# Loading the first group's keys of a fused attention and feed-forward kernel in two transfers

## The chip, the cores and the metric

The kernel runs on one core of a Trainium2 chip. The metric is the device time of one execution in microseconds (us). Beside it stands a profile of one execution, taken by the hardware profiler, whose span reaches from the core's first to its last instruction.

## The reference

Two stages, the second fed by the first. B, H, S, D are 8, 12, 448 and 64; the second stage has 3584 rows (8 x 448), a width of 768 (12 x 64) and a hidden width of 2048.

```python
scores = scale * np.matmul(q, k.transpose(0, 1, 3, 2)) - np.log(S)
attn = 1.0 / (1.0 + np.exp(-scores))
attn_out = np.matmul(attn, v)
x = attn_out.transpose(0, 2, 1, 3).reshape(B * S, H * D)
h = x @ w_in
out = (h * (1.0 / (1.0 + np.exp(-beta * h)))) @ w_out
```

Inputs and output are float32. The attention has no softmax: each score goes through a sigmoid by itself.

## The kernel before

Work is in groups of four heads, three groups a batch, 24 in all. A group's queries and keys lie in a tile `raw` of 128 partitions: each of the four heads owns 32 partitions, and each partition holds 14 consecutive rows of 64 values ("blocks", NB = 14). VectorE (DVE) transposes these in squares of 32 x 32 into `qT` (L200) and `kT` (L212); TensorE (PE) makes scores from them (L229), ScalarE (ACT) puts the sigmoid on them (L242, L257), PE multiplies with the values (L335), DVE copies the result to `xT` (L349), and the feed-forward layers follow from there, partly as sums of products with fewer multiplications (L379, L410, L524, L652). Results leave by SyncE's queue (L711). The order of instructions on every engine is written out by hand: the lists LOADS, LATER, BEGIN (L811 to L881) and UNITS set it.

Nearly all loads are issued by GpSimd (POOL), which also converts float32 to float16 on the way (L125, L154, L169). The exception is group 0, whose keys and first half of the queries go as float32 on SyncE's (SP's) queue into `staged`, a piece of the later tile `gt` that is still free (L820 to L827): keys first, 14 blocks of 64 float32 values in each of 128 partitions, 448 KB, then 7 blocks of queries, 224 KB. The third transfer on that queue is beta, 8 KB (L856). At the same time POOL begins with the list LOADS: keys of group 1, the other half of group 0's queries, queries of group 1, values and so on.

BEGIN then has, in this order: the cast of key blocks 0 to 7 to float16 on DVE (L835), of key blocks 8 to 13 on ACT (L833) and of the 7 query blocks on ACT (L833); on DVE the key transposes, one over blocks 0 to 7 and one over blocks 8 to 13 (L212), and the transpose of the first half of the queries (L200); on PE 20 matmuls on a zeroed tile that compute nothing of use ("idle", L849), then the scores of group 0 for the first half of the queries, with further such matmuls between ("busy", L854). The DVE transposes of beta (L868) stand behind the queries of group 1.

The split of the keys at block 8 is that of `rows_of`:

```python
def rows_of(i: int):
    n = JF + int(i < KL // BLK)
    return i * JF + min(i, KL // BLK), n
```

With JF = 3 and KL // BLK = 2, `rows_of(0)` is (0, 4): four blocks from block 0.

Of the kernel before, what the change touches and what calls it, by code (L numbers as in the profile page):

```python
# [13 lines left out]
def kernel(  # L14
# [14 lines left out]
    B, H, S, D = q.shape  # L29
# [4 lines left out]
    HQ = P // BLK  # L34
    NB = S // BLK
# [106 lines left out]
# [4 lines that stand above are left out]
# [644 lines left out]
    NH = NB // 2  # L790
    share_psum(3)
    with tc.manual_schedule():
# [27 lines left out]
        staged = gt[:, 0:4].rearrange("p c w -> p (c w)").bitcast(FP32)  # L820
        raws[0] = rawp.tile([P, 2, NB, D], FP16, tag="raw", name="raw")
        parts = {1: (staged, NB), 0: (staged[:, NB * D :], NH)}
        for r, (to, n) in parts.items():
            nc.sync.dma_start(
                out=to[:, 0 : n * D],
                in_=(q, k)[r][0, 0:HQ].rearrange("h (p c) d -> (h p) (c d)", c=NB)[:, 0 : n * D],
            )  # L827

        def cast(r: int, c0: int, c1: int, act: bool):
# [234 lines left out]
```

## Time and profile before

| what | value |
|---|---|
| time, median of 3 runs | 369.52 us (369.27 to 369.52) |
| time of the profiled execution | 369.46 us |
| its span | 367.7 us |
| PE busy | 362.2 us, 99% |
| DVE busy | 262.7 us, 71% |
| ACT busy | 258.5 us, 70% |
| POOL busy | 83.4 us, 23% |
| moved by DMA | 34.62 MB, mean 94 GB/s |
| packets of POOL's queue (q0) | 26400, 40.5% of the 16 engines' span |
| packets of SyncE's queue (q1) | 5984, 11.6% of the 16 engines' span |

How to read it: the time holds some 1.8 us around the span. "Busy" counts the stretches in which an engine has an instruction under way; matmuls are pipelined, so a PE that is busy all the time is not one at its peak. L with a number is a line of the kernel. The DMA engines are shared: one transfer's rows are spread over all 16, and each row of a transfer is a packet or more.

### The profile page before, as it was taken

The numbers are of one execution on the slowest core, as the hardware profiler recorded it, in microseconds if no ns is written. First come the engines' busy times: TensorE is split into PE (matmuls) and PEld (weight loads), VectorE is DVE, ScalarE is ACT, GpSimd is POOL, SyncE is SP. The second block draws the span as 40 slices with busy tenths as digits, with TensorE's granted clock in tenths as the row PEclk, the third lists the DMA queues.
The fourth block names the chain that finished last, engine by engine and source line by source line (L and its number), as shares of the span: only waits on it lengthen the run. The fifth ranks groups of instructions, "written<-read, shape, count | busy, mean of one in ns | idle before, by whom it ended". The sixth has DMA issues, their size and how long they took to land.

```text
span 367.7 us, 7007 instructions
## 1 busy us (share of the span) xinstructions
PE 362.2 (99%) x2756; PEld 175.9 (48%) x2756; DVE 262.7 (71%) x487; ACT 258.5 (70%) x306; POOL 83.4 (23%) x125
## 2 busy tenths in 40 slices
PE   8999999999999999999999999999999999999996
PEld 4434444434444455544444455554444455555664
DVE  3548765688988867785675976779766677687664
ACT  5987976999777588876877759887777758870000
POOL 7525343311310023331131003337000012210000
PEclk9999999999999999999999999999999999999999
DMA  8999999955292110096379221004903030002332
GB/s 166 204 207 202 205 205 202 225 65 89 40 167 57 44 45 1 1 170 140 52 128 167 55 50 37 1 2 68 214 34 86 2 87 0 1 2 65 89 102 89
DMA packets 32416, 34.62 MB, mean 94 GB/s; under 512 B 9328, under 2 KB 28416, under 8 KB 32384
## 3 DMA queue, kind: packets, MB, share of 16 engines
q0 software_dynamic: 26400, 22.47, 40.5%
q1 hardware_dynamic: 5984, 11.71, 11.6%
q8 instruction: 21, 0.34, 0.4%
q14 instruction: 11, 0.09, 0.1%
HBM read 45.62 MB, written 11.01 MB: 154 GB/s over the span
## 4 chain that ended last, share of the span: by engine, by line
PE 92%; DMA 3%; DVE 2%; ACT 1%; issue 0%; DVEq 0%; ACTq 0%
PE ps L652 34%; PE ps L524 26%; PE ps L229 12%; PE ps L335 10%; PE ps L379 6%; PE ps L410 3%; DMA raw<-in_q_dram 2%; PE ps L854 1%; ACT attns L257 1%; DMA gt<-in_k_dram 1%; DVE w_S L484 1%; DVE gt L397 0%; ACT attns L242 0%; DVE qT L200 0%; ACT sg L396 0%
## 5 line engine op out<-in xcount | busy, mean ns | idle before, releaser
L257 ACT ACTIVATE attns<-ps,nlogs 128x1792 f16<-128x1792 f32 x73 | 128.0, 1754 | 41.0 <-PE ps L229 40.8
L652 PEld LDWEIGHTS <-sum 128*128 128x128 f16 x536 | 48.9, 98 | 42.1 <-issue 13.7
L652 PE MATMUL ps<-w_T,sum 128*128 128x384 f16 (+2 forms) x328 | 58.1, 319 | 0.0
L538 POOL TENSOR_TENSOR gt<-attns,sg 128x448 f16<-128x448 f32 x21 | 23.9, 1137 | 146.0 <-ACT sg L535 146.0
L229 PE MATMUL ps<-qT,kT 32*128 32x448 f16 (+3 forms) x800 | 50.5, 353 | 1.1 <-ACT attns L242 0.5
L535 ACT ACTIVATE sg<-ps,beta_sb 128x448 f32<-128x448 f32 x72 | 45.1, 630 | 8.6 <-PE ps L524 5.9
L524 PE MATMUL ps<-xT,w_in 128*128 128x448 f16 x216 | 49.2, 353 | 0.0
L524 PE MATMUL ps<-xT,w_S 128*128 128x448 f16 x216 | 49.2, 352 | 0.0
L538 DVE TENSOR_TENSOR gt<-ps,sg 128x448 f16<-128x448 f32 x72 | 44.3, 619 | 2.3 <-ACT sg L535 2.2
L349 DVE CAST xT<-ps 128x448 f16<-128x448 f32 (+1 forms) x50 | 27.9, 599 | 25.2 <-PE ps L335 25.2
L671 DVE TENSOR_TENSOR osb<-ps,osb 128x384 f32<-128x384 f32 (+2 forms) x67 | 36.1, 540 | 12.1 <-PE ps L652 10.5
L524 PEld LDWEIGHTS <-w_in 128*128 128x128 f16 x288 | 28.0, 98 | 26.6 <-issue 0.7
L379 PE MATMUL ps<-xT,w_in 128*128 128x448 f16 x192 | 40.0, 353 | 0.0
L335 PE MATMUL ps<-attns,v 128*64 128x448 f16 (+3 forms) x400 | 39.9, 353 | 0.0
L638 DVE TENSOR_TENSOR sum<-gt 128x1024 f16<-128x1024 f16 x57 | 38.4, 690 | 0.2
L652 PE MATMUL ps<-w_out,sum 128*128 128x384 f16 x208 | 37.9, 327 | 0.0
L652 PE MATMUL ps<-w_out,gt 128*128 128x384 f16 (+2 forms) x200 | 36.6, 320 | 0.0
L585 DVE TENSOR_TENSOR ps<-ps,attns 128x448 f32<-128x448 f32 x24 | 15.2, 633 | 24.1 <-PE ps L524 24.1
L524 PEld LDWEIGHTS <-w_S 128*128 128x128 f16 x216 | 21.1, 98 | 19.4
L125 POOL DMA_DIRECT2D raw<-in_q_dram x24 | 13.3, 555 | 67.7 <-DVE kT L212 53.2
L379 PEld LDWEIGHTS <-w_in 128*128 128x128 f16 x192 | 17.5, 98 | 21.2 <-issue 6.8
L335 PEld LDWEIGHTS <-v 128*64 128x64 f16 (+1 forms) x400 | 17.8, 108 | 20.4 <-issue 13.0
(57 smaller groups left out, 345.8 us busy)
## 6 DMA issues: line engine op xcount, KB each, us to landing
out_dram<-osb SPq DMA_DIRECT2D x98, 96.0 KB, 1.9
raw<-in_k_dram POOLq DMA_DIRECT2D x23, 224.0 KB, 6.5
raw<-in_q_dram POOLq DMA_DIRECT2D x23, 224.0 KB, 6.0
v<-in_v_dram POOLq DMA_DIRECT2D x16, 192.0 KB, 7.7
w_out<-in_moe_w_out_dram POOLq DMA_DIRECT2D x4, 768.0 KB, 17.9
v<-in_v_dram POOLq DMA_DIRECT2D x16, 144.0 KB, 8.0
w_in<-in_moe_w_in_dram POOLq DMA_DIRECT2D x3, 512.0 KB, 11.0
w_in<-in_moe_w_in_dram POOLq DMA_DIRECT2D x3, 256.0 KB, 11.4
```

Source lines behind the costliest of these rows:

```text
L229: nc.tensor.matmul(sco[base : base + nk, hh, u0 : u0 + n], kT[g][lo : lo + BLK, jt * P : jt * P + nk, e], qT[g][lo : lo + BLK, c0 : c0 + n ...
L257: nc.scalar.activation(out=attns[:, slot : slot + 2].rearrange("p n h s -> p (n h) s"), in_=sco, func=AF.Sigmoid, bias=nlogs[:, 0:1], scal ...
L335: nc.tensor.matmul(av[hh * D : (hh + 1) * D, 0:n], vs[b][base : base + nk, 2 * (s % NPAIR) + hh, jt], at[base : base + nk, hh, 0:n], start ...
L349: nc.vector.tensor_copy(out=xTs[b][:, s % NPAIR, c0 : c0 + n], in_=av)
L379: nc.tensor.matmul(m1, w_in16[:, hc, dc * P : (dc + 1) * P], xTs[b][:, hc], start=fresh, stop=(hc == hi - 1), skip_group_check=lo > 0,)
L524: nc.tensor.matmul(out, w[:, c, i * P : (i + 1) * P], m[:, c], start=(start and c == 0), stop=(c == KH - 1), skip_group_check=not start,)
L535: nc.scalar.activation(out=sg, in_=h, func=AF.Sigmoid, bias=0.0, scale=beta_sb[:, dc : dc + 1])
L538: return lambda: engine.tensor_tensor(out=gt[:, dc, b % 2 * S : b % 2 * S + S], in0=h, in1=sg, op=ALU.mult)
L585: nc.vector.tensor_tensor(out=D, in0=B, in1=p5, op=ALU.add)
L638: nc.vector.tensor_tensor(out=sums[t, i], in0=x, in1=y, op=op)
L652: nc.tensor.matmul(m2, (x if op is None else sums[t, i])[:, dc], w[:, dc, lo:hi], start=first, stop=(dc == ND - 1), skip_group_check=i >= 4,)
L671: nc.vector.tensor_tensor(out=out, in0=in0, in1=in1, op=op)
```

## The change

The keys' transfer is cut at block 8 (K0 = 2 x 4): 8 blocks (256 KB), then 6 blocks (192 KB), then the queries as before. All three are issued by SyncE, in this order, ahead of beta. Nothing else is edited; lines below it move down by one.

```diff
         parts = {1: (staged, NB), 0: (staged[:, NB * D :], NH)}
-        for r, (to, n) in parts.items():
+        K0 = 2 * rows_of(0)[1]
+        for r, c0, c1 in ((1, 0, K0), (1, K0, NB), (0, 0, NH)):
             nc.sync.dma_start(
-                out=to[:, 0 : n * D],
-                in_=(q, k)[r][0, 0:HQ].rearrange("h (p c) d -> (h p) (c d)", c=NB)[:, 0 : n * D],
+                out=parts[r][0][:, c0 * D : c1 * D],
+                in_=(q, k)[r][0, 0:HQ].rearrange("h (p c) d -> (h p) (c d)", c=NB)[:, c0 * D : c1 * D],
             )
```

The instructions that read these tiles stay in number and order. The waits follow the transfers: DVE's cast now waits for the first part of the keys, ACT's first cast for the second part.

## The prediction

> **What bounds the kernel now.** I read the page first, for who is busy, then the first 20 us of the timeline, because the edit touches nothing later, then the waits, and last the DMA view in narrow windows, because the edit changes only transfers.
>
> ```profile
> PE 362.2 (99%) x2756; PEld 175.9 (48%) x2756; DVE 262.7 (71%) x487; ACT 258.5 (70%) x306; POOL 83.4 (23%) x125
> PE ps L849 <- DVE gt L843: 1.2, 1, 1.2
> PE ps L229 <- ACT attns L242: 0.5, 1, 0.5
> PE ps L229 <- DVE qT L200: 0.4, 1, 0.4
> ```
>
> The page's first row has TensorE (PE) busy for 99% of the span. The other three rows are all of PE's waits in the whole trace: 2.1 us. Only one of them lies between the loads of group 0 and PE: the 0.4 us for the transposed queries. So the start of the first scores sets the time: what moves it moves the rest, unless something later absorbs it. The timeline of the start, in the order in which it is needed:
>
> ```profile
> 0.74 0.38 SPq L824 DMA_DIRECT2D gt<-in_k_dram  x1
> 1.18 0.42 SPq L824 DMA_DIRECT2D gt<-in_q_dram  x1
> 1.65 0.42 SPq L856 DMA_DIRECT2D beta_in<-in_moe_beta_dram  x1
> 1.29 0.72 POOL L125 DMA_DIRECT2D raw<-in_k_dram  x1 [0.42 <-issue]
> 1.19 4.27 PE L849 MATMUL ps<-gt 128*128 128x256 f16 x20 [1.19 <-DVE gt L843]
> 4.25 0.43 DVE L835 CAST raw<-gt 128x512 f16<-128x512 f32 x1 [2.99 <-DMA gt<-in_k_dram]
> 4.25 1.13 ACT L833 CAST raw<-gt 128x384 f16<-128x384 f32 x2 [2.02 <-DMA gt<-in_k_dram]
> 4.81 0.56 ACT L833 CAST raw<-gt 128x448 f16<-128x448 f32 x1
> 4.71 0.70 DVE L212 STREAM_TRANSPOSE kT<-raw 128x256 f32<-128x256 f32 x2
> 5.41 0.41 DVE L200 STREAM_TRANSPOSE qT<-raw 128x224 f32<-128x224 f32 x1
> 5.88 0.70 PE L229 MATMUL ps<-qT,kT 32*128 32x224 f16 x16 [0.41 <-DVE qT L200]
> 6.29 14.67 ACT L242 ACTIVATE attns<-ps,nlogs 128x448 f16<-128x448 f32 x17 [0.91 <-PE ps L229]
> ```
>
> Columns are start, duration, engine and line, and in brackets the idle time before and what ended it. The keys land, VectorE (DVE) casts blocks 0 to 7 and ScalarE (ACT) blocks 8 to 13; ACT then casts the queries (4.81 for 0.56, so until about 5.38). DVE transposes the keys until 5.41 and then the queries, and PE starts at 5.88. At 5.41 two conditions meet: DVE is through with the keys, and ACT ended its second cast 0.03 us before. The same 0.03 lies between DVE's cast (ends 4.68) and its first transpose (4.71), so ACT's cast of the queries is by itself enough to hold the query transpose at 5.41. Ahead of the scores PE only runs 20 idle matmuls, until 5.46, so no earlier arrival can win more than the 0.41 us in brackets.
>
> When the transfers land, by the DMA view (KB each, us from issue to landing):
>
> ```profile
> gt<-in_k_dram SPq DMA_DIRECT2D x1, 448.0 KB, 3.5
> gt<-in_q_dram SPq DMA_DIRECT2D x1, 224.0 KB, 3.6
> beta_in<-in_moe_beta_dram SPq DMA_DIRECT2D x1, 8.0 KB, 4.2
> out_dram<-osb SPq DMA_DIRECT2D x98, 96.0 KB, 1.9
> ```
>
> Keys: 0.74 + 3.5 = 4.2. Queries: 1.18 + 3.6 = 4.78, just ahead of ACT's 4.81. beta: 1.65 + 4.2 = 5.85. That is the row to stop at: 8 KB, third on SyncE's queue, land 1.07 us after the queries although they were issued 0.47 us after them, while stores of 96 KB take 1.9 in the median. Something came between the second and the third transfer. The DMA view cut at 3.8 us names it:
>
> ```profile
> DMA packets 218, 0.59 MB, mean 156 GB/s; under 512 B 15, under 2 KB 90, under 8 KB 218
> q1 hardware_dynamic: 218, 0.59, 51.5%
> ...
> q0 software_dynamic: 197, 0.27, 91.0%
> ...
> 0.00:1.70 1.70, 0.74 (x7) 1.00 0.00 0
> 1.70:3.80 2.10, 2.10 (x5) 1.00 0.93 282
> ```
>
> The last two rows are stages of POOL, with DMA share and GB/s in the last columns: no data moves before 1.70. The first two rows are of the window 0 to 3.8: all 218 packets are SyncE's (q1), none is POOL's (q0). The third is of 3.8 to 5.9: POOL's packets now take 91% of the 16 engines. POOL had issued its first load at 1.29. How long such an issue takes to reach idle engines is seen where DMA rests:
>
> ```profile
> 80.29 0.58 POOL L125 DMA_DIRECT2D raw<-in_q_dram  x1 [9.11 <-DVE xT L349]
> ...
> 80.25:81.50 1.25, 1.25 (x8) 0.69 (x7) 1.11 (x2) 1.25 (x1) 1.12 (x2) 1.00 0.00 0
> 81.50:82.00 0.50, 0.50 (x7) 0.12 (x8) 0.00 (x0) 0.50 (x2) 0.00 (x0) 1.00 1.04 68
> ```
>
> Nothing until 81.50, then packets, some 1.2 us or a little more after the issue. By that POOL's load of 1.29 stood ready at about 2.5 to 2.7, and still moved nothing until 3.8, when the queries' packets ran out. My reading, an inference: engines serve work in the order in which it reached them. Keys and queries reached them before POOL's load did and went through whole; beta, issued at 1.65, reached them with POOL's load or after it and had to share.
>
> **The change part by part.** *Removed and added.* One issue of 448 KB becomes two of 256 and 192 KB. No wait is added on any engine; the instruction order of PE, DVE, ACT and POOL stays, and SyncE has one more issue. Its cost there is the spacing of the rows above, 1.18 - 0.74 = 0.44 or 1.65 - 1.18 = 0.47.
>
> *The first keys.* 192 of 448 KB no longer stand ahead of DVE's cast. Their packets run from 1.70 to at most 4.2, 2.5 us, and 192 of 448 parts of that are 1.07: 256 KB may land near 3.2; at worst they gain nothing. DVE's cast and the first key transpose move ahead by as much. The second key transpose needs ACT's cast of blocks 8 to 13, which ends by 4.81, so the key transposes end near 4.81 + 0.03 + half of 0.70 = 5.2 in place of 5.41. That 0.2 us is worth nothing: the next thing on DVE needs ACT's cast of the queries, which ends at 5.38 at the earliest.
>
> *The last keys.* The bytes ahead of them are the same. The packets double, from 8 to 16 on each engine (128 rows over 16 engines). A packet's fixed cost lies between nothing and the mean of one in the mixed window above (51.5% of 16 x 3.8 us over 218 packets: 0.14 us, 8 of them 1.1 us); since those packets are long and their time goes with bytes I take nothing.
>
> *The queries.* They are now third on SyncE's queue, issued at 1.18 + 0.44 to 0.47 = 1.62 to 1.65: the slot and the moment of beta before. Two prices. By beta's row they land at 1.62 + 4.2 = 5.82, which is 1.04 later than 4.78. By packets: if one POOL packet goes between each two rows of the queries, 8 rows an engine wait for 8 packets of 91.0% x 16 x 2.1 us / 197 = 0.155 us, 1.24 us. If they keep their place it is nothing, and if only the issue delay passes on, 0.44. I take 1.1, near beta's row, for it is the same slot of the same queue. A second row supports the size: the eight stores issued around 62 to 67 us, when POOL's queue is full, take this long,
>
> ```profile
> out_dram<-osb SPq DMA_DIRECT2D x8, 96.0 KB, 5.2
> ```
>
> against 1.9 in the median of all such stores: behind POOL's work a SyncE transfer loses up to 3.3 us.
>
> The Trainium skill, page "DMA: Bandwidth & Descriptors", section "Queues, rings and completion order", says that each engine goes round-robin between its queues, packet by packet. The row of the window 0 to 3.8 does not agree for keys and queries, as POOL's load seems to have been ready; beta's row does. By the rule alone the queries after the change share with POOL, and the sum would be that of the 1.24 us.
>
> *From there to the end.* Queries cast by ACT from 5.9, transposed from 6.5, scores at 5.88 + 1.1 = 7.0. ACT's sigmoids run without a break from 6.29 for 14.67 us and PE shows no wait of its own in this stage but the 0.5 us for them; both begin later by 1.1 and nothing in between has slack:
>
> ```profile
> 5.88:21.96 16.08, 16.08 (x198) 1.00 1.24 198
> 40.00:364.00 324.00, 323.89 (x2422) 1.00 0.45 81
> ...
> 9.28 0.80 DVE L868 STREAM_TRANSPOSE beta_sb<-beta_in 32x32 f32<-32x32 f32 x4
> ```
>
> The first two are PE's busy time by stage: 16.08 of 16.08 us and 323.89 of 324. So the delay is passed on whole. beta, now fourth, landed at 5.85 and is needed at 9.28 by the last row; that cover of 3.4 us hides its delay, and if POOL's queue holds it as it held the stores (3.3 us) just about still.
>
> *Sum.* The profiled execution took 369.46 (span 367.7), the median of the runs is 369.52, 0.06 higher. 369.46 + 1.1 = 370.56, so 370.6.
>
> **The rivals.**
>
> *Queries keep their place (not slower).* One mechanism, at the DMA engines' queues: if q's rows arrive before POOL's first load, they go through whole as before. The point that decides is whether 1.62 to 1.65 on SyncE beats 1.29 on POOL. For it: POOL's issue there took 0.72 against 0.58 at 80 us, so POOL may be late. Against it: beta, issued at the same moment, did not pass. Then the keys' last part still lands near 4.2, ACT's casts stay where they are, and the time is 369.5; with the issue delay of 0.44 passed on, 369.9. All of this lies within 0.2% (0.74 us), about what a measurement of this kernel can tell from no change.
>
> *The gain arrives (faster).* If the split also spread the keys better over the engines, so that ACT got its blocks and the queries earlier, PE could start when its idle matmuls end: 0.41 earlier at most, 369.05. Against it: the bytes ahead of the queries are the same, and they are last.
>
> *More than beta's delay.* Every POOL packet between the rows and then some slow first packets, or PE's wait of 0.41 + 1.1 = 1.5 us costing the granted clock, 1.00 until now: 371.0 to 371.8. A relative of it: each transfer pays its own landing in sequence, which by the stores' row is 1.9, 371.4. Against that stands that the queries landed only 0.56 us after the keys. The Trainium skill, same page, section "Anatomy of one DMA — SWDGE (gpsimd) path", gives a fixed cost of about 2.0 us a transfer for POOL's path; in sequence that would be, as an estimate from that page, 371.5, and the 0.56 disagrees.
>
> **How the numbers follow.** Queries behind POOL's packets: 0.68, 370.1 to 371.1 (0.7 to 1.6 us). They keep their place: 0.20, 369.4 to 369.9. Some gain: 0.05, 369.05 to 369.4. More than beta's delay: 0.07, 371.0 to 371.8. The likeliest gives 370.6. Both signs' cases are needed for 8 in 10, so the range goes from 369.4 to 371.2; the likeliest alone would be 370.1 to 371.1. Slower by over 0.2% (above 370.2): most of the first case and the last, 0.70. Faster by over 0.2%: even the cap of 0.41 does not reach it, 0.02 for the spread of the runs on top. The rest, 0.28, is the same.
>
> **What would show it.** Right: the DMA view has the 256 KB landing well before 4.2 and the queries at about 5.8, with POOL's packets in the stretch where the queries' run; DVE's cast near 3.4; PE's wait for the query transpose near 1.5 in place of 0.41; from 7.0 on the same rows, all shifted by one amount. Wrong at its root: queries landing by 4.9 and PE starting at 5.9. Wrong only later: PE starting near 7.0 with an end that moved less, which would mean slack between that I did not see.

## The result and the profile after

The changed kernel takes 374.75 us (median of 5 runs, 373.25 to 375.3), the kernel before 369.49 (369.27 to 369.52): a ratio of 1.0137, with a 95% interval of 1.0115 to 1.016. It is 5.3 us slower. The prediction was slower by 1.1 (370.6, range 369.4 to 371.2). The profiled execution took 375.07, with a span of 373.3 against 367.7, so 5.6 us are to be found in it.

The DMA view of the changed kernel, for the transfers that the prediction turned on (KB each, us from issue to landing):

```profile
gt<-in_k_dram SPq DMA_DIRECT2D x1, 256.0 KB, 2.6
gt<-in_q_dram SPq DMA_DIRECT2D x1, 224.0 KB, 6.6
gt<-in_k_dram SPq DMA_DIRECT2D x1, 192.0 KB, 2.7
beta_in<-in_moe_beta_dram SPq DMA_DIRECT2D x1, 8.0 KB, 6.3
```

The first keys land at 0.74 + 2.6 = 3.3 and the last keys at 1.17 + 2.7 = 3.9, both earlier than the 4.2 of the whole before. The queries, issued at 1.64, land at 8.2 in place of 4.78. The timeline shows what that does:

```profile
0.74 0.84 SPq L825 DMA_DIRECT2D gt<-in_k_dram  x2
1.64 0.42 SPq L825 DMA_DIRECT2D gt<-in_q_dram  x1
1.19 3.85 PE L850 MATMUL ps<-gt 128*128 128x256 f16 x20 [1.19 <-DVE gt L844]
3.41 0.56 DVE L836 CAST raw<-gt 128x512 f16<-128x512 f32 x1 [2.14 <-DMA gt<-in_k_dram]
3.87 0.51 ACT L834 CAST raw<-gt 128x384 f16<-128x384 f32 x1 [1.63 <-DMA gt<-in_k_dram]
4.00 0.79 DVE L212 STREAM_TRANSPOSE kT<-raw 128x256 f32<-128x256 f32 x2
8.25 0.56 ACT L834 CAST raw<-gt 128x448 f16<-128x448 f32 x1 [3.88 <-DMA gt<-in_q_dram]
8.85 0.70 DVE L200 STREAM_TRANSPOSE qT<-raw 128x224 f32<-128x224 f32 x2 [4.06 <-ACT raw L834]
9.31 1.08 PE L229 MATMUL ps<-qT,kT 32*128 32x224 f16 x16 [4.27 <-DVE qT L200]
```

The keys are transposed by 4.8 instead of 5.41, and it wins nothing: DVE then stands idle for 4.06 us until ACT has cast the queries. PE starts its scores at 9.31, which is 3.43 later than 5.88. The last row holds a second loss: the same 16 matmuls now take 1.08 us, before 0.70. PE's busy time by stage (stage, its length, busy, granted clock, DMA share, GB/s) says why:

```profile
0.00:5.00 5.00, 3.81 (x20) 1.00 0.55 128
5.00:7.50 2.50, 0.05 (x1) 1.00 1.10 201
7.50:9.30 1.80, 0.00 (x0) 0.56 1.31 191
9.30:14.00 4.70, 4.68 (x40) 0.50 1.36 182
14.00:16.00 2.00, 2.00 (x24) 0.87 1.14 209
16.00:22.00 6.00, 6.00 (x81) 1.00 1.19 208
```

PE has nothing to do from 5.0 to 9.3, the granted clock goes to 0.50, and it stays there until past 14. Before, the column read 1.00 in all these stages, and the 16 matmuls took 0.70. So the 5.6 us are 3.43 of a late start and 2.2 after it.

Where the queries' time went is in the DMA view, cut at two windows. First the changed kernel from 3.46 (the first row of queries) to 5.46, then from 5.46 to 7.75 (packets, MB, share of the 16 engines):

```profile
DMA packets 145, 0.25 MB, mean 125 GB/s; under 512 B 5, under 2 KB 145, under 8 KB 145
q0 software_dynamic: 76, 0.13, 51.8%
q1 hardware_dynamic: 69, 0.12, 20.0%
...
q0 software_dynamic: 308, 0.34, 96.1%
q1 hardware_dynamic: 107, 0.12, 17.2%
```

In the first window POOL and SyncE move about as many packets, 76 and 69, while the engines are far from full (52 + 20%) and move 125 GB/s. In the second, POOL has three packets for one of SyncE's, counted over all engines. Before, no packet of POOL's moved until 3.8, and the queries landed at 4.78. They did share their end: SyncE's row of the window 3.8 to 5.9 in the kernel before, which the prediction does not show, is

```profile
q1 hardware_dynamic: 102, 0.10, 15.1%
```

That is more than beta's 8 KB, so the last of the queries ran beside POOL's packets there too. That POOL's first loads begin slowly is no effect of the change: the kernel before, with POOL nearly alone from 4.45 to 5.9 and then in full flow from 10 to 14, shows

```profile
DMA packets 162, 0.19 MB, mean 134 GB/s; under 512 B 23, under 2 KB 162, under 8 KB 162
q0 software_dynamic: 153, 0.19, 97.6%
...
DMA packets 1194, 0.81 MB, mean 203 GB/s; under 512 B 767, under 2 KB 1194, under 8 KB 1194
```

### The profile page after: what moved, and what is told of

It is laid out like the page before. It is cut to its first block, busy times and chain, and to the rows that moved or that the text cites. A ratio compares the mean times of both kernels' runs of the same rounds, so it can differ in the third digit from the quotient of the medians.

```text
span 373.3 us, 7011 instructions
## 1 busy us (share of the span) xinstructions
PE 364.1 (98%) x2756; PEld 176.1 (47%) x2756; DVE 262.8 (70%) x487; ACT 259.1 (69%) x306; POOL 84.1 (23%) x125
## 4 chain that ended last, share of the span: by engine, by line
PE 95%; DMA 2%; ACT 2%; issue 1%; DVE 0%; SPq 0%; ACTq 0%
PE ps L652 33%; PE ps L524 26%; PE ps L229 12%; PE ps L335 10%; PE ps L379 9%; PE ps L410 3%; PE ps L855 2%; DMA gt<-in_q_dram 2%; ACT attns L257 1%; ACT attns L242 0%; ACT sg L396 0%; SPq L825 0%; DVE osb L671 0%; ACT raw L834 0%; DVE qT L200 0%
## 5 line engine op out<-in xcount | busy, mean ns | idle before, releaser
L229 PE MATMUL ps<-qT,kT 32*128 32x448 f16 (+3 forms) x800 | 51.3, 358 | 4.9 <-DVE qT L200 4.3
L229 PEld LDWEIGHTS <-kT 32*128 32x128 f16 (+1 forms) x800 | 12.9, 97 | 34.4 <-issue 32.6
```

What stands on the lines that cost most here:

```text
L229: nc.tensor.matmul(sco[base : base + nk, hh, u0 : u0 + n], kT[g][lo : lo + BLK, jt * P : jt * P + nk, e], qT[g][lo : lo + BLK, c0 : c0 + n ...
```

## The experiments

Theory: issued at 1.64, the queries come level with POOL's first load and share the DMA engines with it (the place on the queue or the moment of issue decides); the rest is the clock. Rivals: the cut itself (more transfers, more packets) makes SyncE's loads slow; and, for the part after the start, the loss lies in later stages and not in the clock. Unless said otherwise the edits are to the changed kernel. A time without a ratio is that of a single run.

**e1_queries_second.**

```diff
-        for r, c0, c1 in ((1, 0, K0), (1, K0, NB), (0, 0, NH)):
+        for r, c0, c1 in ((1, 0, K0), (0, 0, NH), (1, K0, NB)):
```

> The changed kernel with the order first keys, queries, last keys on SyncE's queue. Place theory (whoever is third on the queue arrives with POOL's first load and has to share with it): queries land near 4.2 to 4.4, the last keys take the lateness, 6 us or more from issue to landing, near 8; PE's first scores near 9.3 to 9.8 and the time 374 to 376. Split theory (two pieces with twice the packets are slow by themselves): the queries stay near 8 or at least beyond 6, whatever their place.

374.85 us. Its DMA view:

```profile
gt<-in_k_dram SPq DMA_DIRECT2D x1, 256.0 KB, 2.7
gt<-in_q_dram SPq DMA_DIRECT2D x1, 224.0 KB, 2.8
gt<-in_k_dram SPq DMA_DIRECT2D x1, 192.0 KB, 6.3
```

The same 224 KB land 2.8 after their issue, and the keys' second part, now third, takes the lateness. Not the queries are slow but whoever is issued third, at 1.64.

**e4_beta_second.** The kernel before, keys whole, with beta's 8 KB between keys and queries (beta's and the constants' memsets move ahead with it):

```diff
         for r, (to, n) in parts.items():
+            if r == 0:
+                nc.sync.dma_start(out=beta_in[0:NDC], in_=moe_beta.rearrange("(c p) -> c p", p=P))
...
-        nc.sync.dma_start(out=beta_in[0:NDC], in_=moe_beta.rearrange("(c p) -> c p", p=P))
```

> The kernel before, keys in one transfer, but beta's 8 KB issued second and the queries third. Place theory: the queries are issued near 1.65 and share with POOL's first load, landing at 6 to 8.5, time 371 to 375.5, although nothing is cut. Split theory: queries land by 5.0 and the time is within 0.3 of 369.5.

375.05 us: the changed kernel's time with nothing cut. Its two rows that matter, beta landing 2.9 after its issue in place of 4.2, and the queries late:

```profile
gt<-in_q_dram SPq DMA_DIRECT2D x1, 224.0 KB, 6.2
...
beta_in<-in_moe_beta_dram SPq DMA_DIRECT2D x1, 8.0 KB, 2.9
```

The cut as such is out.

**e7_keys_on_act and e8_queries_on_act.** Three transfers, none issued late, over two queues. e7:

```diff
-        for r, c0, c1 in ((1, 0, K0), (1, K0, NB), (0, 0, NH)):
-            nc.sync.dma_start(
+        for eng, r, c0, c1 in ((nc.sync, 1, 0, K0), (nc.scalar, 1, K0, NB), (nc.sync, 0, 0, NH)):
+            eng.dma_start(
```

> The changed kernel with the last 192 KB of keys issued on ScalarE's own queue, ahead of its table load, and first keys and queries on SyncE's: three transfers, none issued later than 1.2. Arrival theory: all land by 4.5 ahead of POOL's packets; PE's first scores between 5.46 (its idle matmuls end) and 5.9; time 369.0 to 369.6. If the number of transfers or packets is what costs: 371 or more.

369.61 us, ratio 1.0001 (0.9992 to 1.0009). Its rows:

```profile
gt<-in_k_dram SPq DMA_DIRECT2D x1, 256.0 KB, 3.4
gt<-in_q_dram SPq DMA_DIRECT2D x1, 224.0 KB, 3.6
gt<-in_k_dram ACTq DMA_DIRECT2D x1, 192.0 KB, 3.6
```

The cut, issued in time, costs nothing, and brings nothing: on two queues the keys' parts, both issued at 0.74, land close together, at 4.14 and 4.34, and the queries are transposed from 5.37, before from 5.41. e8 puts the queries on ScalarE's queue and both keys on SyncE's:

> The same with the queries on ScalarE's queue and both parts of the keys on SyncE's, last keys issued at 1.17. Arrival theory: all land by 4.5, PE's first scores between 5.46 and 5.9, time 369.0 to 369.6. If the number of transfers is what costs: 371 or more.

369.90 us, ratio 1.0012 (1.0003 to 1.0021), PE's scores at 6.36: here the last keys are behind the queries (issue 1.17, landing 3.7 later, at 4.87).

**e2_pool_late, e5_pool_later, e13_pool_far_later.** POOL zeroes a piece of a tile that is still free before it issues its first load; n is 1, 2 and 4 (the line is written here once for the three).

```diff
         nc.gpsimd.memset(dummy, 0.0)
+        nc.gpsimd.memset(gt[:, 6 : 6 + n, 0:896], 0.0)
```

> The changed kernel with a memset of 128x896 float16 on POOL ahead of its first load, so that this load starts something like 0.5 to 1 us later. Place theory: the queries go whole ahead of POOL's packets and land by 4.9, PE's first scores start at 5.9 or a little earlier, granted clock 1.00 throughout, time 368.9 to 369.8 unless the later loads miss the delay. Split theory: the queries still land at 6 or later and the time stays above 372.

> The changed kernel with a memset of 128x1792 float16 on POOL ahead of its first load; by the 0.84 us that 128x896 took, that load is issued near 2.4 to 2.5 in place of 1.29, behind the queries' issue at 1.64 by 0.8. Arrival theory (the engines serve the transfers in the order in which they arrive, the queries only lost a race): queries land whole, 2.7 to 3.0 after their issue, by 4.6; PE's first scores at 5.5 to 5.9, clock 1.00, time 369.1 to 369.7. Place theory in its strict form (a third transfer on SyncE's queue always has to wait for POOL): queries land at 5.5 or later, PE after 7, time above 371.

> The changed kernel with a memset of 128x3584 float16 on POOL ahead of its first load, which is then issued near 4.0, long after the queries at 1.64. If POOL's load is what delays the third transfer: queries land whole by 4.5, PE starts by 5.9, clock 1.00; the end may be late by up to 2.7 because all of POOL's loads are. If a third transfer on SyncE's queue is slow by itself: queries land at 5 or later with no POOL packet beside them.

POOL's first load is issued at 1.59, 2.33 and 3.83. The queries' landing, one row of each in this order:

```profile
gt<-in_q_dram SPq DMA_DIRECT2D x1, 224.0 KB, 5.3
```

```profile
gt<-in_q_dram SPq DMA_DIRECT2D x1, 224.0 KB, 3.9
```

```profile
gt<-in_q_dram SPq DMA_DIRECT2D x1, 224.0 KB, 3.4
```

From 6.6 with POOL at 1.29 down to 3.4: POOL's first load makes most of the delay. I had expected "whole" for e2 and e5, which was too sharp. In e2 POOL's issue at 1.59 still lies ahead of the queries' at 1.65. With POOL's issue 0.7 behind theirs (e5) the queries still land at 5.5, not 4.6, and even in e13, where no packet of POOL's moves before 5.2, they take 3.4 against e1's 2.8: these 0.6 have another cause, which no run here shows. Times: 373.86; 371.80 (1.0052, 1.0033 to 1.0071; runs from 370.35 to 372.44, the profiled one the fastest); 371.85. The last is no longer the queries' doing: PE starts at 6.08 there, but waits later for loads of POOL's that come late (0.9 for group 1's keys, 0.8 for values). **e6_before_pool_later** puts a number on that for e5's delay, in the kernel before:

> Control: the kernel before with the same memset, so POOL's loads start 1.1 us later but nothing is cut. If POOL's later loads have slack: 369.3 to 369.7 as before, and beta, third on the queue, lands near 4.9 to 5.1, no longer at 5.85. If the loads are needed early: up to 370.6.

370.01 us (1.0013, 1.0004 to 1.0022), beta landing 3.2 after its issue in place of 4.2. So POOL can't simply be held back.

**e9_rows_not_transfers.** The kernel before, with the keys in one transfer of two rows a partition, one block apart (the key casts are cut at block 7 to match):

```diff
+        nc.sync.dma_start(
+            out=staged[:, 0 : 2 * (NH * D + GAP)].rearrange("p (i w) -> p i w", i=2)[:, :, 0 : NH * D],
+            in_=k[0, 0:HQ].rearrange("h (p i c) d -> (h p) i (c d)", i=2, c=NH),
+        )
...
```

> The kernel before with its keys in one transfer that has two rows of 7 blocks in each partition (with a gap of one block between them in the staging area), so 256 rows as in the changed kernel, but two transfers instead of three; the two key casts are cut at block 7 accordingly. Theory by transfers (the first two transfers of SyncE's queue are taken up by the engines whole, the third takes turns with POOL): queries land by 5.0, beta is the one that is late, PE starts at 5.9 to 6.1, time 369.3 to 369.9. Theory by rows (the engines hold a limited number of rows, about 16 to 18, ahead): queries land at 6 to 8.5 as in the changed kernel, time 372 to 375.

372.64 us; the queries are issued at 1.46 and land late at 6.7 although they are second:

```profile
gt<-in_k_dram SPq DMA_DIRECT2D x1, 448.0 KB, 4.1
...
gt<-in_q_dram SPq DMA_DIRECT2D x1, 224.0 KB, 5.2
```

The theory by transfers falls. Rows ahead can't be all either, since e4 has only beta's small ones. What both share is that the queries are issued later. **e14_queries_late_second** keeps the kernel before, two transfers, same rows. VectorE zeroes the place where the queries land, so that SyncE has to wait before it issues them; the memset of the idle matmuls' tile moves ahead of that:

```diff
+        nc.vector.memset(gt[:, NDC - 1, 0:512], 0.0)
+        nc.vector.memset(staged[:, NB * D : NB * D + NH * D], 0.0)
         for r, (to, n) in parts.items():
...
-        nc.vector.memset(still, 0.0)
```

> The kernel before, two transfers and nothing between them, but VectorE first zeroes the place where the queries land, so that SyncE issues them near 1.6, at the moment at which the changed kernel does. Theory by moment (queries issued at 1.6 come level with POOL's load and share, however few transfers or rows stand ahead): queries land at 6 to 8.5, time 372 to 375. Theory by what stands ahead (8 rows an engine and one transfer, as before): they land by 5.0, time 369.3 to 370.

374.04 us.

```profile
1.64 0.33 SPq L826 DMA_DIRECT2D gt<-in_q_dram  x1
...
gt<-in_q_dram SPq DMA_DIRECT2D x1, 224.0 KB, 5.4
```

Nothing differs ahead of the queries, and they land at 7.0. The moment of issue is enough: 0.46 us later is 2.3 us later in landing. The rest, up to 3.5 in the changed kernel, is in part the spread of single runs: the changed kernel, e3 and e11 issue the same loads at the same times, and their queries land 6.6, 6.1 and 5.8 after issue.

**The clock: e3_more_idle, e11_some_more_idle, e10_before_no_idle.** The count in ("idle", 20) becomes 58 and 44 in the changed kernel, and 1 in the kernel before.

> The changed kernel with 58 idle matmuls ahead of the scores in place of 20, so that PE is busy until about 9 us. Clock theory (beside the 3.4 us by which PE starts late, some 2 us are the granted clock at 0.50 from 7.7 to 14.5, for PE had nothing to do from 5.0 to 9.3): clock 1.00 up to the end, time 369.5 + 3.4 = 372.9, 1.5 to 2.3 less than the changed kernel. If the clock costs nothing: 374.7 as the changed kernel.

> The changed kernel with 44 idle matmuls, which end near 7.5, before the queries land near 8, so that PE is not held by them and has a gap of only 1 to 2 us. Clock theory: clock 1.00, the time is that of before plus the late start, 369.5 + 2.9 to 3.4 = 372.4 to 372.9. If the gap alone, however short, brings the clock down: 374 to 375.

> The kernel before with 1 idle matmul ahead of the scores in place of 20; loads and start of the scores are as before, but PE has done nothing until 5.88. Clock theory (a half clock in the first microseconds of scores costs about 2 us whatever the loads do): granted clock 0.50 from 5.9 for 3 to 7 us, PE still starts at 5.9, time 371.3 to 371.9. If the clock is not what costs in that stage, because ScalarE's sigmoids bind: 369.5 to 369.8.

The first scores of e11, e3 and e10, a row of each:

```profile
8.54 0.70 PE L229 MATMUL ps<-qT,kT 32*128 32x224 f16 x16 [0.79 <-DVE qT L200]
```

```profile
10.09 0.70 PE L229 MATMUL ps<-qT,kT 32*128 32x224 f16 x16
```

```profile
5.88 1.07 PE L229 MATMUL ps<-qT,kT 32*128 32x224 f16 x16 [4.29 <-DVE qT L200]
```

With PE kept busy, the 16 matmuls take 0.70 again, and the span grows by just the late start: e11 starts 2.66 later and its span is 370.3, 2.6 longer; e3 starts 4.21 later (its idle matmuls end after the queries were ready) and is 371.8, 4.1 longer. Medians 372.75 (1.0089, 1.0075 to 1.0103) and 373.55 (1.0092, 1.0066 to 1.0119). In e10 the scores begin at 5.88 as before, at 1.07, and its span is 369.7, 2.0 longer, 371.54 us (1.0053, 1.0039 to 1.0067), with nothing else changed. So the half clock is the 2 us.

The column of the granted clock must be read together with the matmuls' durations, for it reads 1.00 from the first microsecond of every run. The same idle matmuls take 0.22 us each in a run of 20 in 4.45 us, and 0.15 in e11's 44 in 6.55: they begin at half speed, and PE comes to full speed only after some microseconds of work. In e10 PE had done next to no such work, so its scores began slow without any drop. The same holds for e1, e2 and e14, whose 20 idle matmuls took 4.45: PE had not reached full speed when its gap began. First e14, then e6, where the idle matmuls are as slow but no gap follows:

```profile
1.19 4.45 PE L850 MATMUL ps<-gt 128*128 128x256 f16 x20 [1.19 <-DVE gt L823]
8.15 1.08 PE L229 MATMUL ps<-qT,kT 32*128 32x224 f16 x16 [2.51 <-DVE qT L200]
```

```profile
1.19 4.45 PE L850 MATMUL ps<-gt 128*128 128x256 f16 x20 [1.19 <-DVE gt L844]
5.72 0.78 PE L229 MATMUL ps<-qT,kT 32*128 32x224 f16 x16
```

In e6 PE goes on working and is at full speed within its first scores; in e14 the gap puts that off. In the changed kernel, e4 and e9 the idle matmuls took 3.85, 3.92 and 3.78, so PE had reached full speed, and there the column does fall to 0.50 in the gap. e9 has the shortest such gap:

```profile
6.00:8.00 2.00, 0.20 (x8) 0.89 1.21 200
7.79 1.07 PE L229 MATMUL ps<-qT,kT 32*128 32x224 f16 x16 [2.83 <-DVE qT L200]
```

A mean of 0.89 over 2 us is 0.44 us at half, so the clock fell at 7.56, some 2.6 us after PE's last idle matmul at 4.97.

**e12_queries_first.** An attempt at a better version: two transfers, queries ahead of keys, and their cast and transpose first.

```diff
-        for r, (to, n) in parts.items():
+        for r, (to, n) in ((0, parts[0]), (1, parts[1])):
...
-            ("cast", 1, 0, 8, False), ("cast", 1, 8, 14, True), ("cast", 0, 0, 7, True), ("k", 0), ("q", 0, 0),
+            ("cast", 0, 0, 7, True), ("q", 0, 0), ("cast", 1, 0, 8, False), ("cast", 1, 8, 14, True), ("k", 0),
```

> A version that uses what the runs showed: two transfers as before, but queries first and keys second, and the query cast and transpose ahead of those of the keys on ScalarE and VectorE. Only the keys' cast and transpose then stand behind the last landing (4.2): PE's first scores at 5.5 to 5.7, 0.2 to 0.4 earlier than before, time 369.1 to 369.4. If the last landing moves by as much or POOL's load comes in: 369.5 or more.

369.81 us, ratio 1.0021 (1.0000 to 1.0041), two of eleven runs at 371.66 and 373.4: the expected gain did not come. The keys land 3.7 after their issue at 1.17, at 4.87 and not at 4.2, and PE starts at 6.12. No version of this study beats the kernel before.

## Why the prediction was wrong

- *What bounds the kernel, and that a late start is passed on whole.* Right: e11 and e3 moved the start by 2.66 and 4.21 and the span by 2.6 and 4.1.
- *The earlier keys are worth nothing.* Right: transposed by 4.8, and DVE waits for the queries' cast. DVE's cast came at 3.41, forecast near 3.4. That the keys' last part "still lands near 4.2" was wrong by 0.3, without effect.
- *The queries take beta's slot and share with POOL's first load.* Right: whoever is issued near 1.64 shares (e1, e4, e14), and POOL's first load makes most of the delay (e2, e5, e13). One reading under it was wrong: the queries' packets had not run out at 3.8 in the kernel before, as SyncE's 0.10 MB after 3.8 show.
- *"I take 1.1, near beta's row"*. This is the step that failed, by its size: the queries' delay, put at 1.1, measured 8.24 - 4.78 = 3.46. Beta's row was the wrong measure: beta is 8 KB, and the queries have 224 KB in 128 rows, 8 an engine, each of which can have to wait. The upper end, 8 POOL packets of 0.155, had the right form for the first window (76 to 69, about one to one) and the wrong price: 16 engines x 2.0 us over 69 packets of SyncE's is 0.46 us from one to the next on an engine. 0.155 was the time for which a POOL packet keeps an engine busy, and the queries came on at a slower pace than that, with engines to spare (52 + 20%); why, no run here shows. In the second window POOL has three packets for one. The trace of before had shown POOL's slow start (134 GB/s from 4.45 to 5.9), but not this pace: there POOL's packets kept the engines 97.6% busy, 0.15 us each.
- *"Every POOL packet between the rows and then some slow first packets, or PE's wait of 0.41 + 1.1 = 1.5 us costing the granted clock"*, 0.07 for at most 1.2 more than forecast. Both came, and together they were larger than that. The clock term, put only at the edge of the range, is 2.0 to 2.2 us. Its condition was an idle PE, and the wait grew with the queries' delay: 4.27 us, not 1.5. At the forecast 1.5 the traces show none: e5 and e8, with waits of 1.51 and 1.48, keep the 0.70. "1.00 until now" was also a misreading of the column, for in the kernel before the 20 idle matmuls take 4.27, 0.21 each, so that PE comes to full speed just ahead of its scores. The Trainium skill, page "TensorE: Matmul & The Clock Gate", section "Part 1: The HAM clock gate (the "warmup" mystery)", has the clock at half after an idle window of about 3.4 us and back after about as long of sustained work. The half clock is as said. The idle length is shorter here: the clock falls some 2.7 us after PE's last idle matmul in the changed kernel (a mean of 0.56 from 7.5 to 9.3 puts the fall at 7.7, the matmul ended at 5.04) and 2.6 us in e9. It is back 5.2 us after the scores begin in the changed kernel (a mean of 0.87 from 14 to 16 puts it at 14.5).
- *beta's later landing costs nothing.* Right: 2.10 + 6.3 = 8.4, and its DVE transposes moved to 10.55 with everything else.

What stays open: how the engines come to let POOL in, and why the queries then come on so slowly. The moment of issue is enough (e14), neither the count of transfers nor that of rows ahead explains all (e9, e4), but e5 and e13 show some lateness although POOL's load was issued well after the queries. That the spread of the changed kernel (373.25 to 375.3) and of e12 comes from this race, or from whether PE has reached full speed, is argued, not shown. The kernel before has late runs too: 370.6 and 372.21 among the nine that ran beside e1 to e4.

## What to carry to other kernels

Before putting another transfer ahead of a needed one, look at when the needed one will be issued and at what other queues start in that moment; here 0.46 us of issue time turned into 2.3 us of landing with nothing else changed (e14) and 3.5 in the changed kernel. The price of sharing is the pace at which the needed rows move in the stretch where the sharing happens, not the time for which one packet keeps an engine busy. A wait on TensorE in a stage that brings its clock up by filler work can have two prices, the wait and the half clock behind it, whether the gap loses the clock or puts off its rise; the second is tested by adding or taking away filler, and read from the matmuls' durations and not from the clock's column alone.

## What the runs showed of the hardware

Two transfers issued on SyncE's queue by 1.18 went past POOL's load of 1.29 in the kernel before, POOL's first packet coming at 3.8 and less than half of the queries running beside it (0.10 of 0.23 MB); a transfer issued at 1.46 (e9) or 1.64 (changed kernel, e1, e3, e4, e11, e14) never did, landing 5.2 to 6.6 after issue against 2.8 to 3.6. Two transfers issued at 0.74 on SyncE's and ScalarE's queues landed 3.4 and 3.6 after issue (e7), where the first, the same 256 KB, took 2.6 in the changed kernel. TensorE's first matmuls ran at half speed (0.22 us each for the 20 of e14, 0.15 on the mean for the 44 of e11) while the clock's column read 1.00. Once it was at full speed, a gap of 2.83 us (e9) brought the granted clock to 0.50, and gaps of 1.5 (e5, e8) did not.
